# A recurrence with a two-layer feed-forward: a 64-byte carry buffer in a pool of its own, and the last sums of a token pair copied out one unit later

## The chip, the cores and the metric

The kernel runs on one core of a Trainium2 chip. The metric is the device time of one execution in microseconds (us); shorter is better. The work of one core is spread over five engines, each with its own queue of instructions that it takes strictly in the order in which they stand: TensorE (PE in the profile, with its weight loads apart as PEld), VectorE (DVE), ScalarE (ACT), GpSimd (POOL) and SyncE (SP), which here only issues the transfers between DRAM and the on-chip memory.

## What is computed

The input x has 4 sequences of 6080 tokens with 256 features. A recurrence runs along each sequence, and each of its outputs goes through two matrix products with a squared ReLU between them, 2048 hidden values wide.

```python
sig = 1.0 / (1.0 + np.exp(-f_logit))
f = lower_bound[None, None, :] + (1.0 - lower_bound[None, None, :]) * sig
i = 1.0 - f
for t in range(S):
    h = f[:, t] * h + i[:, t] * x[:, t]
    y[:, t] = h
...
h = np.maximum(x @ w_in, 0.0)        # x is y as 24320 x 256
return (h * h @ w_out).astype(np.float32)
```

## The kernel before

**Tiles.** Features lie on the 128 partitions (two halves, `KD` = 2) and tokens along the free axis. The 24320 tokens are cut into 24 pairs of blocks, 512 tokens a block and 384 in the last pair; `j` is the pair, `t` the block in it. The hidden values are cut into 16 slices of 128, and two slices make a unit `q` (`NQ` = 8 units a pair). Every product is made of three matmuls, since each operand is split into a high and a low part: low weight by high data, high by high, high by low (lines 281 to 285 for layer 1, 303 to 305 for layer 2).

**Stages.** The first two pairs go through `plain` (line 321), while the weights are unpacked and the sums of weights that the later pairs need are formed. Pairs 2 to 23 go through `quad` (line 362 on), once for each unit. It makes the four blocks of hidden values of a unit from seven products P1 to P7 in place of eight (a Strassen-like scheme), in four accumulators `a`, `b`, `c`, `d` of the matmul memory.

**Order of a unit.** The order is written out by hand (`tc.manual_schedule`), so each engine's queue holds its instructions as the code issues them. On TensorE a full unit is 45 matmuls: P1 (3 matmuls, into `a`), P5, P7, then the first part of layer 2 of the unit before it, `layer2(*before, 0, 0)` (6 matmuls), then P6 into `d`, P2, P4, P3, and the other three parts of layer 2 of the unit before, `(1, 0)`, `(0, 1)` and `(1, 1)` (18 matmuls). On ScalarE a unit is: the copy `d<-a` of P1 (line 372), on which P6 adds up; the copy of P5 into `s` (line 376); the copy `ghi<-c` of `tail12` of the unit before (line 356), which the layer-2 part `(0, 1)` needs; steps of the next pair's recurrence that `slots` hands out (a sigmoid, line 112, or a split, line 177); the ReLUs and squares of lines 397 to 417.

**The accumulators of layer 2.** `acc_t[j, t]` holds the two result halves of block `t`. Units 0 to 7 of a pair add to them, but since layer 2 runs one unit late, the last addition of pair `j-1` is in unit 0 of pair `j`. `store(j-1, t)` (line 307) then copies the two halves with ScalarE into one buffer, `osb` (line 312), and SP sends that buffer to DRAM (line 313). `osb` has one buffer for both blocks (`bufs=1`), so the copies of block 1 must wait until the transfer of block 0 has landed. Both calls stand at the end of unit 0 (lines 426 and 430; for pair 2, whose predecessor went through `plain`, lines 434 and 435).

**Pools.** The tile pools lie one behind the other in the on-chip memory in the order in which they are entered: `const` (weights), `xA` (split inputs of the even pairs), `ld` (loads, the carry, sums), `hid` (hidden values), `outp` (`osb`); `xB` (split inputs of the odd pairs) is put at the other end. `carry[j]`, 8 bytes a partition, holds the last state of a pair for the recurrence of the next; it has two buffers in `ld`, each on a step of 32 bytes.

Of the kernel before, what the change touches and what calls it, by code (L numbers as in the profile page):

```python
# [8 lines left out]
F32 = mybir.dt.float32  # L9
# [5 lines left out]
P = 128  # L15
# [17 lines left out]
def scan_then_relu2_kernel(  # L33
# [28 lines left out]
    KD = D // P  # L62
    WW = 2 * D
    NQ = KF // 2
# [3 lines left out]
    ld = ctx.enter_context(tc.tile_pool(name="ld", bufs=1))  # L68
    hid = ctx.enter_context(tc.tile_pool(name="hid", bufs=1))
    outp = ctx.enter_context(tc.tile_pool(name="outp", bufs=1))  # L70
    ps = ctx.enter_context(tc.tile_pool(name="ps", bufs=1, space=bass.MemoryType.PSUM))

    xTv = xT.rearrange("(c p) t -> p c t", p=P)
# [16 lines left out]
    x_t, f_t, carry = {}, {}, {}  # L90
# [10 lines left out]
    def segments(t0, n):  # L101
        a = 0
        while a < n:
            s = (t0 + a) % seq
            m = min(n - a, seq - s)
            yield a, m, s == 0
            a += m
# [21 lines left out]
    def op_scan(j, t, c):  # L129
        t0, n = pairs[j]  # L130
        x = x_t[j, t]
        if t == 1 and c == 0:
            carry[j] = ld.tile([P, KD], F32, tag="carry", name=f"carry{j}", bufs=2)
        for a, m, new in segments(t0 + t * n, n):
            if new:
                init = 0.0
            elif a:
                init = x[:, c, a - 1 : a]
            elif t:
                init = x_t[j, 0][:, c, n - 1 : n]  # L140
            else:
                init = carry[j - 1][:, c : c + 1]
            nc.vector.tensor_tensor_scan(
                out=x[:, c, a : a + m], data0=f_t[j, t][:, c, a : a + m],
                data1=x[:, c, a : a + m], initial=init, op0=ALU.mult, op1=ALU.subtract,
            )
        if t == 1 and c == KD - 1 and j + 1 < NP:
            nc.vector.tensor_copy(carry[j][:, :], x[:, :, n - 1])
# [128 lines left out]
    def product(j, q, k, bank, start):  # L277
        n = pairs[j][1]
        hi, lo = whi[q][:, COLUMN[k]], wlo[q][:, COLUMN[k]]
        r = RIGHT[k]  # L280
        for m, (w, x) in enumerate(((lo, xhi), (hi, xhi), (hi, xlo))):
            nc.tensor.matmul(  # L282
                bank[:, :n], lhsT=w, rhs=x[j, r][:, :n], start=start and m == 0, stop=m == 2,
                skip_group_check=True,
            )
# [4 lines left out]
    def layer2(j, q, h, t):  # L290

        t0, n = pairs[j]
        if (j, t) not in acc_t:
            acc_t[j, t] = [
                ps.tile([P, NB], F32, tag=f"acc{t}{d}", name=f"acc{j}_{t}_{d}") for d in range(KD)
            ]
        ghi, glo = g_t.pop((j, q, h, t))
        first, last = q == 0 and h == 0, q == NQ - 1 and h == 1
        for d in range(KD):
            col = (5 if h else 9) + d  # L300
            hi, lo = whi[q][:, col], wlo[q][:, col]
            acc = acc_t[j, t][d][:, :n]
            nc.tensor.matmul(acc, lhsT=lo, rhs=ghi[:, :n], start=first, stop=False)  # L303
            nc.tensor.matmul(acc, lhsT=hi, rhs=ghi[:, :n], start=False, stop=False)  # L304
            nc.tensor.matmul(acc, lhsT=hi, rhs=glo[:, :n], start=False, stop=last)  # L305

    def store(j, t):
        t0, n = pairs[j]
        a = t0 + t * n
        osb = outp.tile([P, KD, NB], F32, tag="osb", name=f"osb{j}_{t}")  # L310
        for d in range(KD):
            nc.scalar.activation(out=osb[:, d, :n], in_=acc_t[j, t][d][:, :n], func=AF.Copy)  # L312
        nc.sync.dma_start(out=outTv[:, :, a : a + n], in_=osb[:, :, :n])
# [33 lines left out]
    def tail12(j, q):  # L347

        n = pairs[j][1]
        c12 = c12_t.pop((j, q))  # L350
        ghi, glo = pair_of(j, q, 0, 1)
        c = c12[:, :n]
        nc.vector.scalar_tensor_tensor(  # L353
            out=c, in0=c, scalar=0.0, in1=c, op0=ALU.max, op1=ALU.mult
        )
        nc.scalar.activation(out=ghi[:, :n], in_=c, func=AF.Copy)  # L356
        yield
        nc.vector.tensor_tensor(  # L358
            out=glo[:, :n], in0=c, in1=ghi[:, :n].bitcast(F32), op=ALU.subtract
        )  # L360

    def quad(j, q, before, slots):


        n = pairs[j][1]

        a, b, c, d = (
            ps.tile([P, NB], F32, tag=k, name=f"{k}{j}_{q}") for k in ("abcd" if q % 2 else "acbd")
        )
        av, bv, cv, dv = (k[:, :n] for k in (a, b, c, d))  # L370
        product(j, q, "P1", a, True)
        nc.scalar.activation(out=dv, in_=av, func=AF.Copy)  # L372
        product(j, q, "P5", c, True)
        s = hid.tile([P, NB], F32, tag="s", name=f"s{j}_{q}")
        sv = s[:, :n]
        nc.scalar.activation(out=sv, in_=cv, func=AF.Copy)  # L376
        product(j, q, "P7", b, True)
        nc.vector.tensor_tensor(out=sv, in0=bv, in1=sv, op=ALU.add)  # L378
        left = tail12(*before) if len(before) == 2 else iter(())
        next(left, None)  # L380
        slots(0)
        if len(before) == 2:
            layer2(*before, 0, 0)
        else:
            layer2(*before[0])
        product(j, q, "P6", d, False)
        product(j, q, "P2", a, False)
        product(j, q, "P4", c, False)
        product(j, q, "P3", b, False)
        c22 = hid.tile([P, NB], F32, tag="c22", name=f"c22_{j}_{q}")  # L390
        c22v = c22[:, :n]
        nc.vector.tensor_tensor(out=c22v, in0=dv, in1=sv, op=ALU.add)  # L392
        for _ in left:
            pass
        r11 = hid.tile([P, NB], F32, tag="r", name=f"r11_{j}_{q}", bufs=2)[:, :n]
        hi11, lo11 = (k[:, :n] for k in pair_of(j, q, 0, 0))
        nc.scalar.activation(out=r11, in_=av, func=AF.Relu)  # L397
        r22 = hid.tile([P, NB], F32, tag="r22", name=f"r22_{j}_{q}")[:, :n]
        hi22, lo22 = (k[:, :n] for k in pair_of(j, q, 1, 1, 2))
        nc.scalar.activation(out=r22, in_=c22v, func=AF.Relu)  # L400
        nc.scalar.activation(out=hi11, in_=r11, func=AF.Square)
        nc.vector.tensor_tensor(out=av, in0=av, in1=r11, op=ALU.mult)  # L402
        nc.scalar.activation(out=hi22, in_=r22, func=AF.Square)  # L403
        nc.vector.tensor_tensor(out=cv, in0=c22v, in1=cv, op=ALU.subtract)
        nc.gpsimd.tensor_tensor(out=r22, in0=r22, in1=r22, op=ALU.mult)  # L405
        nc.gpsimd.tensor_tensor(out=lo22, in0=r22, in1=hi22.bitcast(F32), op=ALU.subtract)  # L406
        r21 = hid.tile([P, NB], F32, tag="r", name=f"r21_{j}_{q}", bufs=2)[:, :n]
        hi21, lo21 = (k[:, :n] for k in pair_of(j, q, 1, 0))
        nc.scalar.activation(out=r21, in_=cv, func=AF.Relu)
        nc.vector.tensor_tensor(  # L410
            out=lo11, in0=av, in1=hi11.bitcast(F32), op=ALU.subtract
        )
        c12_t[j, q] = hid.tile([P, NB], F32, tag="c12", name=f"c12_{j}_{q}")
        nc.vector.tensor_tensor(
            out=c12_t[j, q][:, :n], in0=c22v, in1=bv, op=ALU.subtract
        )
        nc.scalar.activation(out=hi21, in_=r21, func=AF.Square)  # L417
        nc.vector.tensor_tensor(out=cv, in0=cv, in1=r21, op=ALU.mult)
        nc.vector.tensor_tensor(  # L419
            out=lo21, in0=cv, in1=hi21.bitcast(F32), op=ALU.subtract  # L420
        )
        if len(before) == 2:
            pj, pq = before
            layer2(pj, pq, 1, 0)
            if pq == NQ - 1:
                store(pj, 0)
            layer2(pj, pq, 0, 1)
            layer2(pj, pq, 1, 1)
            if pq == NQ - 1:
                store(pj, 1)  # L430
        else:
            for late in before[1:LAG]:
                layer2(*late)
            store(j - 1, 0)
            store(j - 1, 1)
        slots(1)


# [87 lines left out]
    with tc.manual_schedule():  # L526
        order = [(j, i, t) for j in range(PLAIN) for i in range(KF) for t in range(2)]
        todo, per = [], 4
        for s, (j, i, t) in enumerate(order):
# [29 lines left out]
            if s >= LAG:  # L559
                pj, pi, pt = order[s - LAG]  # L560
# [8 lines left out]
        for j in range(PLAIN, NP):  # L569
            steps = units(j + 1) if j + 1 < NP else []  # L570
            for q in range(NQ):
                def slots(k):
                    if steps:
                        for o in steps.pop(0):
                            o()
# [7 lines left out]
        j, q = before  # L583
# [45 lines left out]
```

## Time and profile before

| What | Value |
|---|---|
| time, median of 3 runs | 2055.5 us (2054.15 to 2055.97) |
| the profiled execution's own time | 2055.8 us |
| span of its trace, first to last instruction | 2054.0 us |
| TensorE busy | 2002.1 us, 97% of the span |
| VectorE / ScalarE / GpSimd busy | 1536.5 / 1185.6 / 832.6 us |
| granted TensorE clock, mean | 0.997 |
| data moved | 84.69 MB, 41 GB/s on average |

The time of an execution is a little longer than the span (here by 1.8 us). A row of the timeline gives the start in the span, the duration, the engine, the line of the code, the tiles written and read (numbers left out) and, in brackets, how long the engine sat idle before it and what it waited for. A row of the waits gives who waited for whom: us in total, how many times, the longest. Rows of matmuls overlap, as matmuls are pipelined: their starts tell more than their durations.

### The profile page before, as it was taken

How to read it: one execution, taken by the hardware profiler on the slowest of the kernel's cores; microseconds unless marked ns; L12 is line 12 of the kernel's file. 1: busy time of each engine (PE TensorE's matmuls, PEld its weight loads, DVE VectorE, ACT ScalarE, POOL GpSimd, SP SyncE). 2: the span in 40 equal slices, each digit the busy share in tenths (PEclk: the TensorE clock that was granted, in tenths of full speed). 3: DMA queues.
4: the chain of work that ended last, by engine and by line, in shares of the span. 5: the costliest groups of instructions: out<-in, count | busy, mean ns of one | idle time of the engine just before them, and what ended most of it. 6: DMA issues, size and time to landing. Idle time of an engine off the chain costs nothing.

```text
span 2054.0 us, 24632 instructions
## 1 busy us (share of the span) xinstructions
PE 2002.1 (97%) x8688; PEld 1627.1 (79%) x8688; DVE 1536.5 (75%) x2283; ACT 1185.6 (58%) x2127; POOL 832.6 (41%) x712
## 2 busy tenths in 40 slices
PE   5999999999999999999999999999999999999998
PEld 3777787787878877878788787788887877878888
DVE  8975677777777777877778777777787777867765
ACT  4765555556555555555655555556555565555554
POOL 5747243443433424335344343443433424335332
PEclk9999999999999999999999999999999999999999
DMA  4211010101101011010110100101101011010000
GB/s 163 84 62 41 32 32 31 52 11 62 36 27 52 31 42 52 11 62 25 38 52 11 62 32 31 52 12 61 41 22 52 31 41 52 11 59 24 21 21 16
DMA packets 42013, 84.69 MB, mean 41 GB/s; under 512 B 2848, under 2 KB 4384, under 8 KB 41888
## 3 DMA queue, kind: packets, MB, share of 16 engines
q1 hardware_dynamic: 41888, 83.11, 12.1%
q8 instruction: 68, 1.11, 0.2%
q14 instruction: 57, 0.47, 0.1%
HBM read 58.20 MB, written 24.90 MB: 40 GB/s over the span
## 4 chain that ended last, share of the span: by engine, by line
PE 81%; DVE 6%; ACT 6%; DMA 4%; issue 2%; POOL 1%; SPq 0%; ACTq 0%; DVEq 0%; POOLq 0%
PE acc L303 14%; PE acc L305 14%; PE acc L304 14%; PE a L282 10%; PE c L282 10%; PE b L282 10%; PE d L282 6%; DMA out_dram<-osb 3%; ACT osb L312 2%; PE d L335 1%; DVE a L402 1%; DVE c L353 1%; ACT ghi L417 1%; DVE wy L223 1%; DVE c L392 1%
## 5 line engine op out<-in xcount | busy, mean ns | idle before, releaser
L303 PE MATMUL acc<-ghi,wlo 128*128 128x512 f32 (+1 forms) x1536 | 603.7, 393 | 6.1 <-ACT ghi L339 4.9
L305 PE MATMUL acc<-glo,whi 128*128 128x512 f32 (+1 forms) x1536 | 601.3, 391 | 3.3 <-DVE glo L343 3.1
L304 PE MATMUL acc<-ghi,whi 128*128 128x512 f32 (+1 forms) x1536 | 595.6, 388 | 0.0
L405 POOL TENSOR_TENSOR r<-r 128x512 f32<-128x512 f32 (+1 forms) x176 | 181.7, 1032 | 821.4 <-ACT ghi L403 622.7
L305 PEld LDWEIGHTS acc<-glo,whi 128*128 128x128 f32 x1536 | 288.8, 188 | 73.5 <-DVE glo L343 8.2
L303 PEld LDWEIGHTS acc<-ghi,wlo 128*128 128x128 f32 x1536 | 289.0, 188 | 66.0 <-ACT ghi L339 3.6
L304 PEld LDWEIGHTS acc<-ghi,whi 128*128 128x128 f32 x1536 | 288.9, 188 | 62.2
L356 ACT ACTIVATE ghi<-c 128x512 fp32r<-128x512 f32 (+1 forms) x176 | 110.6, 628 | 269.3 <-DVE c L353 269.3
L406 POOL TENSOR_TENSOR glo<-r,ghi 128x512 fp32r<-128x512 f32 (+1 forms) x176 | 226.7, 1288 | 13.8
L372 ACT ACTIVATE d<-a 128x512 f32<-128x512 f32 (+1 forms) x176 | 102.0, 579 | 210.1 <-PE a L282 209.6
L378 DVE TENSOR_TENSOR s<-b,s 128x512 f32<-128x512 f32 (+1 forms) x88 | 60.4, 686 | 215.4 <-ACT s L376 163.9
L182 POOL TENSOR_TENSOR xlo<-T,xhi 128x512 fp32r<-128x512 f32 (+1 forms) x88 | 114.2, 1297 | 137.8 <-ACT xhi L177 137.8
L358 DVE TENSOR_TENSOR glo<-c,ghi 128x512 fp32r<-128x512 f32 (+1 forms) x176 | 156.7, 890 | 2.8 <-ACT ghi L356 0.7
L378 DVE TENSOR_TENSOR s<-c,s 128x512 f32<-128x512 f32 (+1 forms) x88 | 60.3, 686 | 129.5 <-PE c L282 127.5
L182 POOL TENSOR_TENSOR xlo<-x,xhi 128x512 fp32r<-128x512 f32 (+1 forms) x72 | 93.0, 1293 | 146.5 <-ACT xhi L177 145.9
L282 PE MATMUL b<-xhi,wlo 128*128 128x512 f32 (+1 forms) x352 | 138.6, 394 | 0.3 <-DVE glo L419 0.3
L397 ACT ACTIVATE r<-a 128x512 f32<-128x512 f32 (+1 forms) x176 | 103.6, 589 | 61.1 <-PE a L282 61.1
L282 PE MATMUL a<-xhi,wlo 128*128 128x512 f32 (+1 forms) x352 | 138.8, 394 | 0.0
L282 PE MATMUL c<-xhi,wlo 128*128 128x512 f32 (+1 forms) x352 | 138.4, 393 | 0.0
L282 PE MATMUL a<-xlo,whi 128*128 128x512 f32 (+1 forms) x352 | 138.1, 392 | 0.0
L392 DVE TENSOR_TENSOR c<-d,s 128x512 f32<-128x512 f32 (+1 forms) x176 | 119.1, 677 | 24.8 <-PE d L282 20.5
L282 PE MATMUL b<-xlo,whi 128*128 128x512 f32 (+1 forms) x352 | 137.4, 390 | 0.0
(120 smaller groups left out, 4147.5 us busy)
## 6 DMA issues: line engine op xcount, KB each, us to landing
f<-in_fT_dram SPq DMA_DIRECT2D x46, 512.0 KB, 4.5
x<-in_xT_dram SPq DMA_DIRECT2D x46, 512.0 KB, 3.7
out_dram<-osb SPq DMA_DIRECT2D x46, 512.0 KB, 2.8
wraw<-in_wpack_dram SPq DMA_DIRECT2D x15, 512.0 KB, 3.3
f<-in_fT_dram SPq DMA_DIRECT2D x2, 384.0 KB, 3.5
x<-in_xT_dram SPq DMA_DIRECT2D x2, 384.0 KB, 3.2
out_dram<-osb SPq DMA_DIRECT2D x2, 384.0 KB, 2.4
wraw<-in_wpack_dram SPq DMA_DIRECT2D x2, 256.0 KB, 5.6
```

Of the source, the lines that this page charges most:

```text
L182: eng.tensor_tensor(out=xlo[j, i][:, :n], in0=block(j, k), in1=xhi[j, i][:, :n].bitcast(F32), op=ALU.subtract,)
L282: nc.tensor.matmul(bank[:, :n], lhsT=w, rhs=x[j, r][:, :n], start=start and m == 0, stop=m == 2, skip_group_check=True,)
L303: nc.tensor.matmul(acc, lhsT=lo, rhs=ghi[:, :n], start=first, stop=False)
L304: nc.tensor.matmul(acc, lhsT=hi, rhs=ghi[:, :n], start=False, stop=False)
L305: nc.tensor.matmul(acc, lhsT=hi, rhs=glo[:, :n], start=False, stop=last)
L356: nc.scalar.activation(out=ghi[:, :n], in_=c, func=AF.Copy)
L358: nc.vector.tensor_tensor(out=glo[:, :n], in0=c, in1=ghi[:, :n].bitcast(F32), op=ALU.subtract)
L378: nc.vector.tensor_tensor(out=sv, in0=bv, in1=sv, op=ALU.add)
L392: nc.vector.tensor_tensor(out=c22v, in0=dv, in1=sv, op=ALU.add)
L397: nc.scalar.activation(out=r11, in_=av, func=AF.Relu)
L405: nc.gpsimd.tensor_tensor(out=r22, in0=r22, in1=r22, op=ALU.mult)
L406: nc.gpsimd.tensor_tensor(out=lo22, in0=r22, in1=hi22.bitcast(F32), op=ALU.subtract)
```

## The change

Two edits. The carry goes from `ld` into a pool of its own, `small`, that is entered after `outp`. So the tiles that lay behind the carry, from the sums in `ld` over all of `hid` to `osb`, lie 64 bytes lower (two buffers of 32 bytes); `const`, `xA`, the load buffers and `xB` stay where they were. And `store(j-1, 1)` is no longer called at the end of unit 0 of pair `j`; it is called in unit 1, behind the copy of P5 into `s` and before P7. `store(j-1, 0)` stays, and so does the end of the last pair.

```diff
@@ pools
     outp = ctx.enter_context(tc.tile_pool(name="outp", bufs=1))
+    small = ctx.enter_context(tc.tile_pool(name="small", bufs=1))
@@ op_scan
-            carry[j] = ld.tile([P, KD], F32, tag="carry", name=f"carry{j}", bufs=2)
+            carry[j] = small.tile([P, KD], F32, tag="carry", name=f"carry{j}", bufs=2)
@@ quad
         nc.scalar.activation(out=sv, in_=cv, func=AF.Copy)
+        if q == 1:
+
+            store(j - 1, 1)
         product(j, q, "P7", b, True)
...
             layer2(pj, pq, 1, 1)
-            if pq == NQ - 1:
-                store(pj, 1)
         else:
             for late in before[1:LAG]:
                 layer2(*late)
             store(j - 1, 0)
-            store(j - 1, 1)
         slots(1)
```

Of the instructions, only the two ScalarE copies of each `store(j-1, 1)` stand elsewhere in their queue, 22 times, once for each pair from 2 to 23. On TensorE, VectorE, GpSimd and SP the rows follow one another as before.

ScalarE's queue before, around the end of unit 0 of pair 12 (`osb11_0` and `osb11_1` are the two blocks of pair 11, `d12_1` the copy of P1 of unit 1 of pair 12, the last number of a name counts buffers):

```order
L417 ACTIVATE ghi12_0_10_9403<-r21_12_0_9402 128x512
L312 ACTIVATE osb11_0_9418<-acc11_0_0_8715 128x512
L312 ACTIVATE osb11_0_9418<-acc11_0_1_8716 128x512
L312 ACTIVATE osb11_1_9434<-acc11_1_0_8768 128x512
L312 ACTIVATE osb11_1_9434<-acc11_1_1_8769 128x512
L372 ACTIVATE d12_1_9442<-a12_1_9439 128x512
L376 ACTIVATE s12_1_9450<-c12_1_9441 128x512
L356 ACTIVATE ghi12_0_01_9456<-c12_12_0_9407 128x512
```

The same place after the change, in which the line numbers are those of the changed kernel:

```order
L421 ACTIVATE ghi12_0_10_9406<-r21_12_0_9405 128x512
L313 ACTIVATE osb11_0_9421<-acc11_0_0_8718 128x512
L313 ACTIVATE osb11_0_9421<-acc11_0_1_8719 128x512
L373 ACTIVATE d12_1_9441<-a12_1_9438 128x512
L377 ACTIVATE s12_1_9449<-c12_1_9440 128x512
L313 ACTIVATE osb11_1_9451<-acc11_1_0_8771 128x512
L313 ACTIVATE osb11_1_9451<-acc11_1_1_8772 128x512
L357 ACTIVATE ghi12_0_01_9459<-c12_12_0_9410 128x512
```

The two copies of `osb11_1` have moved behind `d` and `s`, and stand directly ahead of the copy `ghi12_0_01`.

At pair 2, where the predecessor (pair 1) went through `plain`, ScalarE's queue before:

```order
L312 ACTIVATE osb1_0_1966<-acc1_0_1_1166 128x512
L312 ACTIVATE osb1_1_1970<-acc1_1_0_1197 128x512
L312 ACTIVATE osb1_1_1970<-acc1_1_1_1198 128x512
L372 ACTIVATE d2_1_1978<-a2_1_1975 128x512
L376 ACTIVATE s2_1_1986<-c2_1_1977 128x512
L356 ACTIVATE ghi2_0_01_1992<-c12_2_0_1955 128x512
```

And after the change:

```order
L313 ACTIVATE osb1_0_1969<-acc1_0_1_1169 128x512
L373 ACTIVATE d2_1_1977<-a2_1_1974 128x512
L377 ACTIVATE s2_1_1985<-c2_1_1976 128x512
L313 ACTIVATE osb1_1_1987<-acc1_1_0_1200 128x512
L313 ACTIVATE osb1_1_1987<-acc1_1_1_1201 128x512
L357 ACTIVATE ghi2_0_01_1995<-c12_2_0_1958 128x512
```

The same two copies have moved over the same two rows.

## The prediction

> **What bounds the kernel now.** I read the page first, then the waits, then one boundary between two pairs on two engines' timelines. The page, its span, TensorE's busy time, its granted clock over 40 slices and the chain of waits by line:
>
> ```profile
> span 2054.0 us, 24632 instructions
> PE 2002.1 (97%) x8688; PEld 1627.1 (79%) x8688; DVE 1536.5 (75%) x2283; ACT 1185.6 (58%) x2127; POOL 832.6 (41%) x712
> PEclk9999999999999999999999999999999999999999
> PE acc L303 14%; PE acc L305 14%; PE acc L304 14%; PE a L282 10%; PE c L282 10%; PE b L282 10%; PE d L282 6%; DMA out_dram<-osb 3%; ACT osb L312 2%; PE d L335 1%; DVE a L402 1%; DVE c L353 1%; ACT ghi L417 1%; DVE wy L223 1%; DVE c L392 1%
> ```
>
> TensorE sets the time: 2002.1 of 2054.0 us, and its clock is full throughout. Work that only touches other engines can win no more than TensorE's 51.9 us of idle time. The chain holds a foreign body: the store transfer (3%) and the copies into `osb` (2%). These 5%, about 100 us, are no gain to be had, since TensorE was busy beside most of that chain; what counts is where TensorE stood still. The waits, longest in total first:
>
> ```profile
> DVE s L378 <- ACT s L376: 165.9, 63, 5.9
> ...
> ACT osb L312 <- DMA out_dram<-osb: 73.6, 24, 4.9
> ...
> PEld d L282 <- ACT d L372: 26.3, 22, 2.9
> ...
> PE d L282 <- ACT d L372: 16.9, 22, 2.5
> ```
>
> The last row is the one that matters: TensorE idles 22 times, 16.9 us in all, before the matmuls of P6 into `d`, until ScalarE has copied P1 there. 22 is the number of pairs from 2 to 23. The row of `osb` shows why the copy is late: ScalarE itself sits 73.6 us, 24 times, until a store has landed. ScalarE's timeline at the boundary from pair 11 to 12:
>
> ```profile
> 1064.69 0.63 ACT L417 ACTIVATE ghi<-r 128x512 fp32r<-128x512 f32 x1
> 1065.23 1.07 ACT L312 ACTIVATE osb<-acc 128x512 f32<-128x512 f32 x2
> 1069.18 1.09 ACT L312 ACTIVATE osb<-acc 128x512 f32<-128x512 f32 x2 [2.89 <-DMA out_dram<-osb]
> 1070.15 0.60 ACT L372 ACTIVATE d<-a 128x512 f32<-128x512 f32 x1
> 1070.67 0.60 ACT L376 ACTIVATE s<-c 128x512 f32<-128x512 f32 x1
> 1072.62 0.64 ACT L356 ACTIVATE ghi<-c 128x512 fp32r<-128x512 f32 x1 [1.36 <-DVE c L353]
> ```
>
> The copies of block 0 run at 1065.23; those of block 1 wait 2.89 us for the buffer; `d` and `s` stand behind them and start back to back, with no wait of their own. TensorE's timeline there, the starts of unit 0, of unit 1 and of unit 2 of pair 12 and the place of the stall:
>
> ```profile
> 1056.21 0.40 PE L282 MATMUL a<-xhi,wlo 128*128 128x512 f32 x1
> ...
> 1063.83 0.39 PE L303 MATMUL acc<-ghi,wlo 128*128 128x512 f32 x1
> ...
> 1066.58 0.40 PE L282 MATMUL a<-xhi,wlo 128*128 128x512 f32 x1
> ...
> 1069.81 0.40 PE L305 MATMUL acc<-glo,whi 128*128 128x512 f32 x1
> 1070.81 0.50 PE L282 MATMUL d<-xhi,wlo 128*128 128x512 f32 x1 [0.61 <-ACT d L372]
> ...
> 1077.78 0.40 PE L282 MATMUL a<-xhi,wlo 128*128 128x512 f32 x1
> ```
>
> Unit 0 takes 1066.58 − 1056.21 = 10.37 us for 45 matmuls, 0.230 us a matmul. Unit 1, with as many, takes 1077.78 − 1066.58 = 11.20. So this boundary costs 0.83 us, of which the row names 0.61; the other 0.22 is the refilling of the pipeline (the first matmul after the wait, 1070.81, starts 1.00 after its predecessor, not 0.23).
>
> **The moved copies: what goes.** Each stall costs its named idle time and the 0.22 around it: 16.9 + 22 × 0.22 = 16.9 + 4.8 = 21.7 us. The weight loads give a second way to it. At the same boundary their row is
>
> ```profile
> 1070.81 0.19 PEld L282 LDWEIGHTS d<-xhi,wlo 128*128 128x128 f32 x1 [1.04 <-ACT d L372]
> ```
>
> It names 1.04 us where the boundary costs 0.83, so 0.21 too much; 26.3 us of such waits less 22 × 0.21 = 4.6 is 21.7 again.
>
> The stalls are alike but for a few. The first and the longest:
>
> ```profile
> 232.07 0.50 PE L282 MATMUL d<-xhi,wlo 128*128 128x512 f32 x1 [1.87 <-ACT d L372]
> ...
> 1826.85 0.50 PE L282 MATMUL d<-xhi,wlo 128*128 128x512 f32 x1 [2.48 <-ACT d L372]
> ```
>
> The first is at pair 2, where unit 0 is shorter; the longest is at pair 21. Both are in the 16.9. With the stall gone TensorE would get at `d` when its queue does. For that ScalarE must be in time, and this is read from unit 0 of pair 12, which has no copies ahead of `d`:
>
> ```profile
> 1057.11 0.58 ACT L372 ACTIVATE d<-a 128x512 f32<-128x512 f32 x1 [1.91 <-PE a L282]
> 1057.80 0.60 ACT L376 ACTIVATE s<-b 128x512 f32<-128x512 f32 x1
> 1059.89 0.64 ACT L356 ACTIVATE ghi<-c 128x512 fp32r<-128x512 f32 x1 [1.49 <-DVE c L353]
> ```
>
> There `d` is copied from 0.90 to 1.48 us after the unit's start (1056.21) and `s` is done at 2.19. In unit 1 P6 is due 15 matmuls after the start, at 1069.81 + 0.23 − 1066.58 = 3.46. `d` is then 2.0 us early, and `s`, which P4 wants six matmuls later at 3.46 + 6 × 0.23 = 4.84, is 2.6 us early. The stall goes wholly, and not by a hair.
>
> **The moved copies: what they meet.** They are not made dearer: two copies, 1.09 us of ScalarE, as before. They still need the buffer. Block 0's transfer takes
>
> ```profile
> 1066.32 2.76 DMA out_dram<-osb
> ```
>
> and is unchanged, so the copies start at 1069.18, 2.60 after the unit's start, as now, and end at 3.69. ScalarE's wait there shrinks from 2.89 to about 2.60 − 2.19 = 0.4 us. Behind them in the queue stands `ghi<-c` (line 356), which in an undisturbed unit starts at 1059.89 − 1056.21 = 3.68: it is held up by 0.01 us or so, nothing. It is wanted by the third layer-2 part, which starts 1063.83 − 1056.21 = 7.62 after the unit's start; `ghi` ends at 3.69 + 0.64 = 4.33. The cover is 3.3 us. The same matmul is the first to write the accumulators that the copies read; the copies are done at 3.69, 3.9 us ahead. Of each step that moves, the transfer moves too: SP issues block 1's store when its copies end, now at 1070.27 − 1066.58 = 3.69 and then the same. SP's order does not change, and behind that store stand only the loads issued at the end of the pair. GpSimd and VectorE get `s` earlier than now (the 5.9 us maximum of the wait for `s` goes), and are asked for nothing new. No cost: 0 us.
>
> Should a landing be as late as at pair 21, the longest stall above, ScalarE's row there is
>
> ```profile
> 1825.22 1.08 ACT L312 ACTIVATE osb<-acc 128x512 f32<-128x512 f32 x2 [4.76 <-DMA out_dram<-osb]
> ```
>
> 4.76 of waiting in place of 2.89, so all is 1.87 us later: `ghi` ends at 4.33 + 1.87 = 6.2, still before 7.62. So I let that stall go too.
>
> A rule speaks against the move. The Trainium skill, "PSUM — Partial Sum Buffer", section "Summary: rules for kernel authors", says to evacuate promptly, since that memory is tight; here the sums are taken out later in the code, so by it the next writer could be late and give back as much as is won, up to 21.7 us. The rows above set no such price: the copies end at the same 3.69 us and the next writer comes at 7.62. I go by the rows: 0.
>
> **The carry's pool.** No instruction is added. What changes is where `hid`, the sums and `osb` lie, 64 bytes lower. No row shows these tiles at another place. What rows do show is the other operand: even pairs read `xA`, odd pairs `xB`, two distant places, 21 of 45 matmuls. Pair 12 is even with 10.37; a unit of pair 13 is
>
> ```profile
> 1139.97 0.40 PE L282 MATMUL a<-xhi,wlo 128*128 128x512 f32 x1
> ...
> 1150.34 0.40 PE L282 MATMUL a<-xhi,wlo 128*128 128x512 f32 x1
> ```
>
> 10.37 as well. So I take 0. The bound, an estimate from the same rows: layer 2's last 12 matmuls of unit 0 take (1066.58 − 1063.83) / 12 = 0.229 us, the average is 0.230. Were a place worth such a 1 ns, 24 matmuls in each of 175 units would give 4200 × 1 ns = 4 us, up or down.
>
> **The sum.** 2055.8 − 21.7 = 2034.1 for the profiled execution. It lies 0.3 above the median of 2055.5, so 2033.8 is forecast for a median; I say 2034.
>
> **The rivals.**
>
> *The stall shrinks but another is next.* ScalarE carries the copies and 0.4 us of waiting in unit 1, and something after `ghi` (the ReLUs that feed the next unit's P1 through VectorE) could now be late. Against it: the 2.0, 2.6 and 3.3 us of cover worked out above. For it: no unit before has the two copies between `s` and `ghi`, and no row shows what VectorE, which gets `ghi` and the ReLUs from ScalarE, makes of that. If each of 22 boundaries kept a third of its cost, 7 us would stay: 2041; if half, 2045. Chance 0.08.
>
> *The wait only changes its place.* The Trainium skill, "Perfetto Trace Analysis", section "Optimization Strategy", says that a gap that repeats can mean too few buffers. `osb` has one before and after, so by that the gap should stay. In the trace the gap is ScalarE's wait for the landing, and TensorE's only through the queue order; with `d` ahead, TensorE would have to wait for the landing by another way for nothing to be won. Then the time is 2055.5. Chance 0.03.
>
> *Slower: the landing decides.* If block 0's store lands so late that the moved copies hold `ghi` beyond 7.62, TensorE stalls at layer 2's third part, and the moved copies then hold ScalarE's whole rest of the unit, which they do not today. It decides from 3.3 us beyond the usual landing, 2.76 + 3.3 = 6.1 us. To be slower by over 0.2% (4.1 us, about what a measurement of this kernel can tell from no change) it must give back 21.7 + 4.1 = 25.8, 1.2 us at each of 22 boundaries, landings of 7.3 us and more throughout; the time would be about 2060. The transfers of `osb`:
>
> ```profile
> DMA to landing us min/median/max: 2.4/2.8/6.1
> ```
>
> The median is less than half of it; one of 48 may touch the point. Chance 0.02, with any harm of the shifted tiles in it (6 ns on each of 4200 matmuls would do the same).
>
> **How the numbers follow.** The forecast has 0.87: 0 to 5 us around it for places of tiles and stray landings. The range reaches from 2030 (forecast less 4 for the tiles) to 2041, the first rival's third kept. Faster by over 0.2% means under 2051.4: 0.87 + 0.08 = 0.95. Same: 0.03. Slower: 0.02.
>
> **What would show it.** In the profile after: the row of TensorE waiting for `d` is gone, or down to one or two times; unit 1 of a pair is 10.37 us between starts of `a<-xhi,wlo`; ScalarE's wait for the store goes from 73.6 us to about 73.6 − 22 × 2.5 = 19; the copies into `osb` of block 1 lie between `s` and `ghi<-c`. Wrong would be a new TensorE wait of 20 or more times at layer 2 for `ghi` (line 357 of the changed kernel) or at P1 of the next unit for VectorE, units other than unit 1 longer than 10.37, which would be the tiles' places, or the row of `d` still there.

## The result and the profile after

| | before | after |
|---|---|---|
| time, median, measured on one chip (4 runs each) | 2054.82 us (2053.69 to 2055.97) | 2004.26 us (2003.48 to 2004.76) |
| span of the profiled execution | 2054.0 us | 2003.0 us |
| TensorE busy | 2002.1 us | 1966.7 us |

The ratio of the times is 0.9754 (95% interval 0.9737 to 0.977). The change wins 50.6 us, where 21.7 had been worked out and 2034 forecast; 2004.3 is below the range's low end of 2030. (In one experiment below, at a distance of 32 bytes, the profiled execution ran at a granted TensorE clock of 0.756; its trace is not read and its time left out.)

The page of the kernel after: the span, TensorE's busy time and the two lines of the chain.

```profile
span 2003.0 us, 24632 instructions
PE 1966.7 (98%) x8688; PEld 1628.3 (81%) x8688; DVE 1535.9 (77%) x2283; ACT 1187.3 (59%) x2127; POOL 829.7 (41%) x712
...
PE 93%; DVE 3%; POOL 2%; ACT 1%; DMA 1%; issue 0%; SPq 0%; DVEq 0%; ACTq 0%; POOLq 0%
PE acc L306 17%; PE acc L304 16%; PE acc L305 16%; PE b L283 12%; PE a L283 12%; PE c L283 12%; PE d L283 6%; PE d L336 1%; DVE wy L224 1%; PE b L336 1%; PE c L336 0%; PE a L336 0%; DMA out_dram<-osb 0%; DVE glo L344 0%; DMA f<-in_fT_dram 0%
```

The store has left the chain (DMA 3% to 0%). But TensorE's busy time fell as well, by 35.4 us, with the same 8688 matmuls and the same granted clock (0.997). The prediction does not account for that: by it the moved copies take away idle time of TensorE, not busy time. The waits of the kernel after:

```profile
ACT d L373 <- PE a L283: 250.0, 132, 2.8
...
DVE s L382 <- ACT s L377: 87.2, 48, 3.2
...
ACT osb L313 <- DMA out_dram<-osb: 21.6, 23, 5.1
```

TensorE's wait for `d`, 16.9 us over 22, is gone, and no wait of TensorE at these boundaries took its place; ScalarE's wait for the store fell from 73.6 to 21.6 (19 had been forecast). ScalarE's timeline at the boundary to pair 12, the one shown of before:

```profile
1040.81 1.07 ACT L313 ACTIVATE osb<-acc 128x512 f32<-128x512 f32 x2
1042.91 0.58 ACT L373 ACTIVATE d<-a 128x512 f32<-128x512 f32 x1 [1.04 <-PE a L283]
1043.59 0.60 ACT L377 ACTIVATE s<-c 128x512 f32<-128x512 f32 x1
1044.74 1.09 ACT L313 ACTIVATE osb<-acc 128x512 f32<-128x512 f32 x2 [0.55 <-DMA out_dram<-osb]
1045.71 0.63 ACT L357 ACTIVATE ghi<-c 128x512 fp32r<-128x512 f32 x1
```

`d` no longer waits for anything but its matmuls; the copies still wait 0.55 us for the landing. TensorE's starts of unit 0, 1 and 2 of pair 12, and P6 in unit 1:

```profile
1031.83 0.39 PE L283 MATMUL a<-xhi,wlo 128*128 128x512 f32 x1
...
1042.03 0.39 PE L283 MATMUL a<-xhi,wlo 128*128 128x512 f32 x1
...
1045.43 0.39 PE L283 MATMUL d<-xhi,wlo 128*128 128x512 f32 x1
...
1052.23 0.39 PE L283 MATMUL a<-xhi,wlo 128*128 128x512 f32 x1
```

Unit 1 is as long as unit 0, so the boundary costs nothing. And both take 10.20 us in place of 10.37: 0.2267 us a matmul for 0.2304. Every unit got shorter. Eight units in each of the 21 pairs from 2 to 22 give 21 × 8 × (10.37 − 10.20) = 29 us; with the 22 of the boundaries that is about the whole result.

### The profile page after: what moved, and what is told of

Read it like the earlier page. It is cut to its first block, busy times and chain, and to the rows that moved or that the text cites. A ratio compares the mean times of both kernels' runs of the same rounds, so it can differ in the third digit from the quotient of the medians.

```text
span 2003.0 us, 24632 instructions
## 1 busy us (share of the span) xinstructions
PE 1966.7 (98%) x8688; PEld 1628.3 (81%) x8688; DVE 1535.9 (77%) x2283; ACT 1187.3 (59%) x2127; POOL 829.7 (41%) x712
## 4 chain that ended last, share of the span: by engine, by line
PE 93%; DVE 3%; POOL 2%; ACT 1%; DMA 1%; issue 0%; SPq 0%; DVEq 0%; ACTq 0%; POOLq 0%
PE acc L306 17%; PE acc L304 16%; PE acc L305 16%; PE b L283 12%; PE a L283 12%; PE c L283 12%; PE d L283 6%; PE d L336 1%; DVE wy L224 1%; PE b L336 1%; PE c L336 0%; PE a L336 0%; DMA out_dram<-osb 0%; DVE glo L344 0%; DMA f<-in_fT_dram 0%
## 5 line engine op out<-in xcount | busy, mean ns | idle before, releaser
L304 PE MATMUL acc<-ghi,wlo 128*128 128x512 f32 (+1 forms) x1536 | 595.7, 388 | 6.5 <-ACT ghi L340 4.8
L283 PE MATMUL c<-xlo,whi 128*128 128x512 f32 (+1 forms) x352 | 136.1, 387 | 0.0
L283 PE MATMUL a<-xhi,whi 128*128 128x512 f32 (+1 forms) x352 | 136.1, 387 | 0.0
```

What stands on the lines that cost most here:

```text
L283: nc.tensor.matmul(bank[:, :n], lhsT=w, rhs=x[j, r][:, :n], start=start and m == 0, stop=m == 2, skip_group_check=True,)
```

## The experiments

Two theories stood against each other. **Place**: the 64 bytes by which the sums, the hidden values and `osb` lie lower shorten the distance from matmul to matmul. **Order**: with the stalls gone TensorE stays in a quicker rhythm, so the moved store did both. For the places, the built programs give the addresses. By their remainder over 256 bytes, weights and the split inputs of all pairs lie at 224 before and after; the hidden values lie at 32 before (64 further on) and at 224 after. The time of before in the four series was 2053.0, 2053.7, 2054.6 and 2054.3 us (medians), each beside its own kernels; ratios are against that. Code is shown against the kernel before for the first two experiments and against the kernel after for all others; `...` stands for lines left out.

### The parts, each alone

`e1_pool_only`: only the pool.

```diff
+    small = ctx.enter_context(tc.tile_pool(name="small", bufs=1))
...
-            carry[j] = ld.tile([P, KD], F32, tag="carry", name=f"carry{j}", bufs=2)
+            carry[j] = small.tile([P, KD], F32, tag="carry", name=f"carry{j}", bufs=2)
```

> Only the carry goes into its own pool; both stores stay at the end of unit 0. Theory place (the 64 bytes by which the sums, the hidden values and the store buffer lie lower shorten every matmul's pitch): units of 10.20 us, the wait for the copy of P1 stays at each of 22 boundaries, about 2004 + 22 = 2026 us. Rival order (the pitch falls because the stalls at the boundaries are gone, and so only with the moved store): units of 10.37, 2055 us.

Measured: 2031.16 us, ratio 0.9892 (0.9877 to 0.9906). TensorE's waits for `d` and the starts of units 0, 1 and 2 of pair 12:

```profile
PE d L283 <- ACT d L373: 20.6, 22, 2.7
```

```profile
1046.73 0.39 PE L283 MATMUL a<-xhi,wlo 128*128 128x512 f32 x1
...
1056.93 0.39 PE L283 MATMUL a<-xhi,wlo 128*128 128x512 f32 x1
...
1068.27 0.39 PE L283 MATMUL a<-xhi,wlo 128*128 128x512 f32 x1
```

10.20, and 11.34 with the stall. The pool alone shortens every unit, and all 22 stalls are still there. Order falls. The time lies 5 us above the 2026 that had been expected, since the stalls grew (see "The sum" below).

`e2_store_only`: only the store.

```diff
+        if q == 1:
+            store(j - 1, 1)
...
-            if pq == NQ - 1:
-                store(pj, 1)
...
-            store(j - 1, 1)
```

> Only the second store moves to unit 1; the carry stays where it was. Theory place: units of 10.37 us, no wait for the copy of P1, about 2055 - 22 = 2033 us, which is what was forecast for the whole change. Rival order: units of 10.20, about 2004 us.

Measured: 2032.93 us, ratio 0.99 (0.9885 to 0.9915), with no wait for `d`. Starts of units 0 to 2 of pair 12:

```profile
1044.69 0.40 PE L282 MATMUL a<-xhi,wlo 128*128 128x512 f32 x1
...
1055.06 0.40 PE L282 MATMUL a<-xhi,wlo 128*128 128x512 f32 x1
...
1065.42 0.40 PE L282 MATMUL a<-xhi,wlo 128*128 128x512 f32 x1
```

10.37 and 10.36. The store alone does what the prediction said of it. In this run two landings were late as well: the moved copies waited 2.33 us for their buffer before they started at 479.04, and 2.47 us before 1806.11, and TensorE did not wait behind them.

`e3_gap64`: the whole change, with the 64 bytes put back where the carry lay.

```diff
+            if j == 0:
+                for _ in range(1):
+                    gap = ld.tile([P, 16], F32, tag="gap", name="gap", bufs=1)
+                    nc.vector.memset(gap, 0.0)
             carry[j] = small.tile([P, KD], F32, tag="carry", name=f"carry{j}", bufs=2)
```

> The whole change, and an unused tile of 64 bytes where the carry lay, so that sums, hidden values and store buffer lie as before and only the carry itself lies elsewhere. Theory place: pitch as before, units of 10.37, about 2033 us. Rival carry (the place of the carry itself, between loads and sums, was the cost): 10.20, about 2004 us.

Measured: 2032.13 us, ratio 0.9896 (0.9881 to 0.9911). Unit 0 of pair 12:

```profile
1043.77 0.40 PE L287 MATMUL a<-xhi,wlo 128*128 128x512 f32 x1
...
1054.13 0.40 PE L287 MATMUL a<-xhi,wlo 128*128 128x512 f32 x1
```

10.36. Not the carry's own place counts, but that of what lies behind it.

### Which tiles, and by what measure

`e4_gap32` and `e8_gap128`: the same with `[P, 8]` (32 bytes) and `[P, 32]` (128 bytes).

> The whole change, and an unused tile of 32 bytes where the carry lay: half of the shift. Theory place leaves open where the border lies: 2004 us if half of the shift is enough, 2033 us if not, and a value between or above if the pitch goes with the remainder of the place by 64 bytes, which is 0 here and 32 before and after. Rival order: 2004 us.

> The whole change, and an unused tile of 128 bytes where the carry lay. If the remainder by 128 counts (32 and 64 off were both slow): 2004 us, units of 10.20. If the remainder by 256 or more counts, or the distance as such: 10.3 to 10.4, 2020 to 2040 us.

Measured: 2040.25 us (0.9933, 0.9916 to 0.9949) and 2033.27 us (0.9899, 0.9882 to 0.9915). Unit 2 of pair 12 with 32 bytes:

```profile
1069.76 0.39 PE L287 MATMUL a<-xhi,wlo 128*128 128x512 f32 x1
...
1080.17 0.39 PE L287 MATMUL a<-xhi,wlo 128*128 128x512 f32 x1
```

10.41, the dearest of the three places tried for the hidden values alone; 10.37 at 64 and again at 128. So the measure is not a remainder by 64 or 128. Nor is it an even start by itself: 32 bytes above 224 the hidden values start at a remainder of 0 by 256, and that was the dearest.

`e7_rest64`: 64 bytes behind the last tile that TensorE reads, so that only tiles of the other engines and `osb` move.

```diff
+        if q == 0:
+            gap = hid.tile([P, 16], F32, tag="gap", name="gap")
+            nc.vector.memset(gap, 0.0)
         v = hid.tile([P, 4, P], F32, tag="s", name=f"v{q}")
```

> The whole change, and 64 bytes behind the last tile of the hidden values that TensorE reads: only tiles that VectorE, ScalarE, GpSimd and the stores use lie 64 bytes higher. If the tiles that TensorE reads carry the effect: 2004 us, units of 10.20. If the others do, by traffic of the other engines: 2033 us, 10.37.

Measured: 2003.8 us, ratio 0.9754 (0.974 to 0.9769), as the whole change. The tiles that moved here carry no effect. The sums and two buffers of the ReLUs (`r`) lie ahead of the gap and kept their place, so this run does not test them. That tiles which TensorE reads do carry an effect is shown by the odd pairs of `e5_all32` below, where their inputs are what lies off.

`e12_carry256`: the new pool stays empty; the carry in `ld`, with 192 bytes behind its 64, so that the hidden values lie 256 higher than in the kernel after.

```diff
-            carry[j] = small.tile([P, KD], F32, tag="carry", name=f"carry{j}", bufs=2)
+            carry[j] = ld.tile([P, KD], F32, tag="carry", name=f"carry{j}", bufs=2)
+            if j == 1:
+                gap = ld.tile([P, 48], F32, tag="gap", name="gap")
+                nc.vector.memset(gap, 0.0)
```

> The moved store, with the carry in the load pool as before and 192 unused bytes behind it, so that sums, hidden values and store buffer lie 256 bytes higher than in the changed kernel. Theory remainder by 256: units of 10.20, 2004 us, with no pool for small tiles. Rivals, a longer period or the distance as such: 10.3 to 10.4, 2015 to 2040 us.

Measured: 2003.77 us, ratio 0.9752 (0.9736 to 0.9768). Unit 2 of pair 12:

```profile
1049.42 0.39 PE L286 MATMUL a<-xhi,wlo 128*128 128x512 f32 x1
...
1059.62 0.39 PE L286 MATMUL a<-xhi,wlo 128*128 128x512 f32 x1
```

10.20. The carry may stay where it was: the remainder by 256 counts.

### The remainder itself, or its agreement

`e5_all32`: 32 bytes ahead of the weights. Weights, inputs of even pairs and hidden values move together, the inputs of odd pairs stay.

```diff
+    gap = cpool.tile([P, 8], F32, name="gap")
+    nc.vector.memset(gap, 0.0)
     lb = cpool.tile([P, KD], F32, name="lb")
```

> The whole change, and 32 bytes ahead of the weights, so weights, split inputs of even pairs, hidden values and all between lie 32 bytes higher and keep their distances; the split inputs of odd pairs, at the other end, stay. Theory distance (the matmul's data must lie at the same remainder as its weights and the other operands): even pairs 10.20 a unit, odd pairs slower, as their inputs are now 32 bytes off, 10.3 to 10.4. Theory place (a tile's own remainder by 64 or more counts): all units change, even pairs too.

Measured: 2018.76 us, ratio 0.9827 (0.9812 to 0.9841). Unit 2 of pair 12 (even) and of pair 13 (odd):

```profile
1059.89 0.39 PE L285 MATMUL a<-xhi,wlo 128*128 128x512 f32 x1
...
1070.09 0.39 PE L285 MATMUL a<-xhi,wlo 128*128 128x512 f32 x1
...
1141.83 0.40 PE L285 MATMUL a<-xhi,wlo 128*128 128x512 f32 x1
...
1152.21 0.40 PE L285 MATMUL a<-xhi,wlo 128*128 128x512 f32 x1
```

10.20 for the even pair, 10.38 for the odd. A remainder of 0 is as good as one of 224, if all have it; an odd pair, its inputs 32 off, pays. Agreement counts.

`e6_x64`: 64 bytes ahead of the inputs of even pairs. In even pairs all data agree and lie 64 off the weights.

```diff
+    gap = xA.tile([P, 16], F32, tag="gap", name="gap")
+    nc.vector.memset(gap, 0.0)
     x_t, f_t, carry = {}, {}, {}
```

> The whole change, and 64 bytes ahead of the split inputs of the even pairs: these, the sums, the hidden values and the store buffer lie 64 bytes higher, that is the latter as before the change, and the weights and the inputs of the odd pairs stay. If weights and moving data must agree: even pairs at 10.4 or more, as now both kinds of data are off; odd pairs 10.37. If only the two kinds of data must agree with each other: even pairs 10.20, odd pairs 10.37.

Measured: 2026.45 us, ratio 0.9865 (0.985 to 0.988). The same units of an even and an odd pair:

```profile
1062.52 0.39 PE L285 MATMUL a<-xhi,wlo 128*128 128x512 f32 x1
...
1072.82 0.39 PE L285 MATMUL a<-xhi,wlo 128*128 128x512 f32 x1
...
1145.05 0.40 PE L285 MATMUL a<-xhi,wlo 128*128 128x512 f32 x1
...
1155.42 0.40 PE L285 MATMUL a<-xhi,wlo 128*128 128x512 f32 x1
```

10.30 and 10.37. Neither expectation was met to the letter: with data that agree among themselves the even pair is better than the odd, but the weights 64 off keep it from 10.20. That data agree only among themselves does not help at every distance: at 128 a unit takes 10.46 with all data off the weights (`e9_d128` below) and 10.37 with the hidden values alone off (`e8_gap128`).

The other distances between all data and the weights (`e9_d128`, `e10_d192`, `e11_d32`): a gap in `xA` as in `e6_x64`, and a tile behind the inputs of odd pairs that brings these down to the same remainder. For 128:

```diff
+    gap = xA.tile([P, 32], F32, tag="gap", name="gap")
+    nc.vector.memset(gap, 0.0)
...
+        if j == 3 and len([1 for p, _ in xlo if p == 3]) == len(OPERAND):
+            tail = pool.tile([P, 32], F32, tag="tail", name="tail")
+            nc.vector.memset(tail, 0.0)
```

> The whole change, with all data that TensorE streams (inputs of even and odd pairs, hidden values) at one common remainder, 128 bytes off the weights'. Theory agree (data must agree with the weights too, and any common distance other than a multiple of 256 costs, as 64 did with 10.30 in even pairs): 10.25 to 10.4 a unit in all pairs, 2012 to 2040 us. Rival data-only (the 64 bytes cost for another reason, the data among themselves count): 10.20, 2004 us, or less if this distance suits the weight loads better.

> As the run with 128, with a distance of 192 bytes. Theory agree: 10.25 to 10.4 in all pairs, 2012 to 2040 us. Rival data-only: 10.20 or less, 2004 us or less.

> As the run with 128, with a distance of 32 bytes. Theory agree: 10.25 to 10.4 in all pairs, 2012 to 2040 us. Rival data-only: 10.20 or less, 2004 us or less.

That left open whether agreement is best or only one of several cheap places, so the last three distances followed (`e13_d96`, `e14_d160`, `e15_d224`):

> As the run with 128, with a distance of 96 bytes between the weights' and the data's remainder. Theory agree-is-best (agreement to 256 bytes is the cheapest place, every other distance costs): over 10.20 a unit, 2010 to 2060 us. Rival some-distances (the cost goes up and down with the distance, and agreement is only one of several cheap places): 10.20 or less, 2004 us or less, at one of 96, 160 and 224.

> As the run with 128, with a distance of 160 bytes. Theory agree-is-best: over 10.20 a unit, 2010 to 2060 us. Rival some-distances: 10.20 or less, 2004 us or less, at one of 96, 160 and 224.

> As the run with 128, with a distance of 224 bytes. Theory agree-is-best: over 10.20 a unit, 2010 to 2060 us. Rival some-distances: 10.20 or less, 2004 us or less, at one of 96, 160 and 224.

| Distance of data from weights, bytes | Unit, us | A matmul, ns | Time, us | Ratio to before (95%) |
|---|---|---|---|---|
| 0 (after) | 10.20 | 226.7 | 2004.26 | 0.9754 (0.9737 to 0.977) |
| 32 (`e11_d32`) | not read | | 2055.52 | 0.9998 (0.9989 to 1.0008) |
| 64 (`e6_x64`, even pairs) | 10.30 | 228.9 | | |
| 96 (`e13_d96`) | 10.50 | 233.3 | 2054.64 | 1.0004 (0.9995 to 1.0013) |
| 128 (`e9_d128`) | 10.46 | 232.4 | 2047.79 | 0.9963 (0.995 to 0.9976) |
| 160 (`e14_d160`) | 10.54 | 234.3 | 2062.08 | 1.0041 (1.0026 to 1.0056) |
| 192 (`e10_d192`) | 10.50 | 233.3 | 2055.89 | 1.0007 (0.9998 to 1.0017) |
| 224 (`e15_d224`) | 10.50 | 233.3 | 2054.23 | 0.9997 (0.9987 to 1.0006) |

Unit 2 of pair 12 at the dearest distance, 160:

```profile
1079.98 0.39 PE L288 MATMUL a<-xhi,wlo 128*128 128x512 f32 x1
...
1090.52 0.39 PE L288 MATMUL a<-xhi,wlo 128*128 128x512 f32 x1
```

Agreement is the best of the eight places, and the others do not rise evenly. The sizes were missed: the first three distances had been expected at 2012 to 2040 us and came out at 2047.8 to 2055.9, and 160 lies above the 2060 that had been the upper end. All of these kernels have the moved store: at 160 the place gives back all of the store's 20 us and more. The best that was measured, 2003.8 us, is the kernel after within the measurement; no place of tiles beat it.

## Why the prediction was wrong

**The moved copies: right.** The term of 21.7 us was measured by itself as 2053.0 − 2032.9 = 20.1 (`e2_store_only`); in its trace the 22 units 1 together are 22.4 us shorter than in that of before. Its steps hold in the profile after: the wait for `d` is gone and no other came at the boundaries; the copies stand between `s` and `ghi` and wait 0.55 us where 0.4 was worked out; `ghi` starts 1045.71 − 1042.03 = 3.68 us after the unit's start, to the hundredth the undisturbed value. The rule on prompt evacuation that the prediction took from the Trainium skill set no price here, and the gap did not outlive the change although `osb` still has one buffer.

**The carry's pool: wrong.** The step that failed is "So I take 0", and with it the bound of 1 ns a matmul. What stood in its place is 3.7 ns a matmul (0.2304 − 0.2267), worth 21.9 us while the stalls stay (2053.0 − 2031.2) and 28.6 without them (2032.9 − 2004.3; the two times are of different series, whose times of before differ by 1.8 us, so it is good to about 2 us). Two errors made it:

- The comparison of even and odd pairs was no test of place. Their inputs lie 93952 bytes apart, which is 367 × 256: the same remainder. The two groups compared were alike in just the thing in question. A control has to differ in it, as the odd pairs of `e5_all32` do.
- The bound of 1 ns came from comparing layer 1 with layer 2 inside one unit, both at the slow pace. The fast pace had been in the trace of before, in the first matmuls behind the stall at 1070.81:

```profile
1071.60 0.39 PE L282 MATMUL a<-xhi,wlo 128*128 128x512 f32 x1
...
1073.41 0.39 PE L282 MATMUL b<-xlo,whi 128*128 128x512 f32 x1
```

Eight matmuls in 1.81 us are 0.226 each, with the same instructions that take 0.231 in a unit without a stall, and all of them read inputs at the weights' own remainder. It is a sign, no proof, since behind more than half of the other stalls the slower pace is back within two matmuls or so. But that TensorE could be quicker than 0.2304 on these matmuls was to be seen; the prediction took the even pace for TensorE's own.

**The sum: two parts that help each other.** The parts alone give 21.9 and 20.1, together 42.0; the whole gives 50.6. In `e1_pool_only` the stalls grew, from 16.9 to 20.6 us named: TensorE comes to P6 sooner, while the landing that it waits for through ScalarE keeps its time (ScalarE's wait for the store is 73.6 us in both traces). So the moved store is worth 2031.2 − 2004.3 = 26.9 on top of the pool. The named waits show 3.7 of the 8.6. The lengths of the units 1 show more: the 22 of them are 22.4 us longer in the trace of before than in that of `e2_store_only`, but 29.0 us longer in that of `e1_pool_only` than in that of the kernel after, so 6.5 of the 8.6 lie there. Why a stall costs more than its named wait, and more so at the quicker pace, was not separated, and the last 2 us are within what the series differ by.

**The rivals.** A wait that is next, a gap that only moves, a landing too late: none came at the boundaries. The longest landing in the profile after, 6.4 us, is no test of the last: its store was issued at 126.1 us, in the pairs that go through `plain`, and TensorE's one wait there for `osb`, 1.6 us, was 1.3 us before. Harm by the shifted tiles had been put at 6 ns a matmul as a mishap within a chance of 0.02; a gain of that kind was not among the rivals at all, though the bound was said to hold up and down.

## What to carry to other kernels

A copy that waits for a buffer holds everything behind it in its engine's queue: put it behind what the bounding engine waits for, and check from the rows that its own reader comes later. An edit that moves tiles in memory without adding an instruction is not free: look at the remainders (here by 256 bytes) of the addresses that TensorE reads, weights and data together, and measure the edit alone. When all units run at one even pace, that pace is a measurement of this layout, not the engine's limit.

## What the runs showed of the hardware

The distance from matmul to matmul (512 columns, a weight load each) depended on the places of weights and data in the on-chip memory: 226.7 ns where all have one remainder by 256 bytes, 228.9 to 234.3 ns at the other places tried, each the mean over a unit. It persists beyond the tiles that disagree: before, with only the hidden values 64 bytes off, layer 1's matmuls, whose own operands agree, took 231 ns too (the nine of P1, P5 and P7 of unit 1 of pair 12, from the first row to the second, in the trace of before):

```profile
1066.58 0.40 PE L282 MATMUL a<-xhi,wlo 128*128 128x512 f32 x1
...
1068.66 0.40 PE L303 MATMUL acc<-ghi,wlo 128*128 128x512 f32 x1
```

Which part of the machine makes this was not shown.

The Trainium skill, "SBUF — State Buffer", section "Door 1: The DMA port swizzle (why `[64,N]` ≈ `[32,N]`)", speaks of lines of 16 bytes; by that alone a shift of 64, which is a whole number of lines, should change nothing, and the measure found here is 256. The Trainium skill, "TensorE: Matmul & The Clock Gate", section "Back-to-back issue gap", gives 512 / 2.4 + 2.5, about 216 ns, for the isolated gap between matmuls of 512 columns, and 131 ns for a stream of them with weight loads; no place tried here reached either, the best being 226.7.
